# Decay phases of a linear attention: one integer-shift pass per unit in place of a per-tile subtraction, the absolute value in a buffer of its own, the modality turn planned later

## The chip, the cores and the metric

The kernel runs on one core of a Trainium2 chip (trn2). The metric is the device time of one launch in microseconds (us); the median of three runs of the kernel before is 974.35 us, from 973.89 to 974.85. The engines are named as in the profile: PE is TensorE's matmuls and PEld its weight loads, DVE is VectorE, ACT is ScalarE, POOL is GpSimd and SP is SyncE, which issues DMAs. L529 is line 529 of the kernel.

## The reference

Three stages run one after the other: a linear attention with a complex decay (4 batches, 8 heads, 768 steps, head size 48), a mixture of experts that sends each of 3072 tokens to one of 8 experts, and a dense gated layer. Cut to what matters:

```python
def _attn_ref(q, k, v, a_re, a_im):
    mag = np.sqrt(a_re * a_re + a_im * a_im)
    scale = np.minimum(mag, 0.999) / (mag + 1e-06)
    a_re_n, a_im_n = (a_re * scale, a_im * scale)
    for t in range(S):
        ar, ai = (a_re_n[:, :, t, :, None], a_im_n[:, :, t, :, None])
        new_re = ar * S_re - ai * S_im
        new_im = ar * S_im + ai * S_re
        kv = np.einsum('bhd,bhe->bhde', k[:, :, t], v[:, :, t])
        S_re, S_im = (new_re + kv, new_im)
        y[:, :, t] = np.einsum('bhd,bhde->bhe', q[:, :, t], S_re)

def _moe_ref(x, modality_id, w_gate, modality_bias, w1, w2):
    logits = x @ w_gate + modality_bias[modality_id]
    e_idx = np.argmax(logits, axis=1)
    ...
    h = np.maximum(x[mask] @ w1[e], 0.0)
    out[mask] = gate_w[mask, None] * (h @ w2[e])

def _moe2_ref(x, w_gate, w_val, w_out):
    g = x @ w_gate
    return (g / (1.0 + np.exp(-g)) * (x @ w_val)) @ w_out
```

The kernel doesn't step through time. It sums the logarithm of the decay's size and its angle over time, so that the state between two steps is a product of exponentials, cosines and sines of those sums.

## The kernel before

**Tiles and units.** The attention part works on 24 tiles (b, t): batch b and a chunk t of 128 steps, in the order of t, with the batches inside. `CUTS` groups them into eleven units of 1, 2, 3, 3, 3, 3, 3, 2, 2, 1 and 1 tiles. A tile has 384 columns (8 heads of 48), so a pass over a unit is 384, 768 or 1152 columns wide. Each unit runs through these stages, one function for each:

- `stage_a1` (L414): ACT squares `ai` into `sx`; DVE forms the magnitude (L422), counts values under a bound into `jk` (L425; only the count is used) and sums (L430); ACT takes two logarithms (L433, L436).
- `stage_a2`: ACT's exponentials (L451, and `w` at L454), DVE's ratio and clamp (L457, L460) and the decay's logarithm into `sx` (L464).
- `stage_angle`: ACT's arctangent (L478), in place in `ai`.
- `stage_decay`: PE sums the logarithms over time with a triangular matrix (L489), ACT's exponentials `p` and `r` (L492); the last row of `p` goes through a DMA (L504) and a turn on PE (L507) to `pt` (L510), the decay of a whole chunk.
- `stage_sum` (L516): the phases. For each tile, the phase at the end of the batch's chunk before it is added to the first row of the angles by a DMA that Pool issues (L526). PE sums the angles over time (L529). ACT writes the nearest whole number of turns into `ki` (L533), and DVE subtracts 2 pi times that number (L538) into `tw`. The last row of `tw` goes to DRAM by another DMA of Pool, the carry (L523).
- `stage_trig`: DVE clamps `tw` to just within plus and minus pi, in place (L562); ACT's sine (L565); DVE's absolute value, in place (L571); ACT's cosine (L575), as the sine of pi/2 minus it. So the clamp waits until the carry's DMA has read `tw`, the absolute value waits for the sine, and the cosine for the absolute value.
- `stage_prod`: k times r and q times p (L588), then the products with cosine and sine, `K` and `Q` (L597).
- `attend`: the new state (L614, L621), transposes on PE (L643) and copies on ACT (L380: `tK`, `tQ`, `yT`, `xo`), scores (L656), mask (L661), outputs (L670) and the logits (L684).
- `route`: DVE's choice of an expert (L750 to L758), counts on PE (L769, L771), ranks (L783 to L787) and the scatter by Pool (L794).

**What sets the order.** Each stage gives its instructions to a planner, `Plan`, with an engine, a cost, what they read and write, and, for DMAs, a latency (`lat`). `shapes` says how many buffers each name has. The planner orders all engines' instructions by list scheduling, the earlier in the program first, and emits them at the end; each engine then runs its list strictly in that order. Squares are fixed to ACT, absolute values to DVE and the turn counts to ACT. The costs and latencies in the planner are numbers of its own; they change the order alone.

**Modality.** `load_const` loads the tokens' modality numbers and the biases. A cast on DVE (L1104), a turn on PE (L279) and five passes on DVE (L289 to L293) make `bias`, which the routing of the first unit reads at L750.

**After it.** The first expert's slot (PE L976 and L990, DVE L983, ACT L979) begins while the attention ends; the other seven slots and the dense layer follow, and the change doesn't touch them.

Of the kernel before, what the change touches and what calls it, by code (L numbers as in the profile page):

```python
# [189 lines left out]
def tile_kernel(  # L190
# [130 lines left out]
    units = [order[sum(CUTS[:i]) : sum(CUTS[: i + 1])] for i in range(len(CUTS))]  # L321
    NU = len(units)
    cnt = const.tile([P, NU], F32, name="cnt")
    bad = const.tile([P, 2], F32, name="bad")
# [17 lines left out]
    for r in range(2):  # L342
# [6 lines left out]
        ar=(3, WIDE), ai=(4, WIDE), sx=(3, WIDE), w=(1, WIDE), q=(2, WIDE), k=(2, WIDE), v=(2, [P, CM, H, HB]),  # L349
        p=(1, WIDE), r=(1, WIDE), tw=(1, WIDE), tr=(1, [P, CM, H, 2, D]), jk=(1, WIDE, BF16), ki=(2, [P, DM], I32),  # L350
        tK=(4, [D2, 4, P]), tQ=(5, [D2, 4, P]), am=(3, [P, 4, P]), K2=(2, [P, H, 2, D]),
# [7 lines left out]
    earlyp = early.enter_context(tc.tile_pool(name="earlyp", bufs=1, side="right"))  # L359
    EARLY = ("ar", "ai", "sx", "w", "tw", "jk", "ki")  # L360
    bufs = {}
# [51 lines left out]
    def stage_a1(u):  # L413
        W = len(units[u]) * DM  # L414
        sq, sx, ai, jk = ("ar", u), ("sx", u), ("ai", u), ("jk", u)
# [24 lines left out]
        plan.op("DVE", t_dve(W), f_bad, r=sqs + [sx], w=[jk, ("cnt", u)], new=[("jk", jk)])  # L440
        plan.op("DVE", t_dve(W), f_sum, r=sqs, w=[sx])
        plan.op("ACT", t_act(W), f_la, w=sqs + ["ACT"], table=LOGEXP)
        plan.op("ACT", t_act(W), f_lx, w=[sx, "ACT"], table=LOGEXP)

    def stage_a2(u):
# [21 lines left out]
        plan.op("ACT", t_act(W), f_ri, w=ris + ["ACT"], table=LOGEXP)  # L467
        plan.op("ACT", t_act(W), f_w, r=[sx], w=[w, "ACT"], new=[("w", w)], table=LOGEXP)
        plan.op("DVE", t_dve(W), f_rt, r=ris, w=ais)
# [46 lines left out]
    def stage_sum(u):  # L516
        la, tw = ("ai", u), ("tw", u)
        for c, (b, t) in enumerate(units[u]):
            pk, ck, kk = ("ph", b, t), ("carry", b), ("ki", b, t)
            lc, tc_ = la + (c,), tw + (c,)  # L520

            def f_carry(c=c, b=b):
                gp.dma_start(carry[b], plan[tw][P - 1 : P, c, :])  # L523

            def f_add(c=c, b=b):
                gp.dma_start(plan[la][0:1, c, :], carry[b], accum_op=ALU.add)  # L526

            def f_mm(c=c, pk=pk):
                pe.matmul(plan[pk][:, :DM], tri, plan[la][:, c, :], start=True, stop=True)  # L529

            def f_ki(e, pk=pk, kk=kk):
                if e == "ACT":
                    sc.activation(out=plan[kk], in_=plan[pk][:, :DM], func=AF.Copy, scale=1.0 / TWO_PI)  # L533
                else:
                    ve.tensor_scalar(out=plan[kk], in0=plan[pk][:, :DM], scalar1=1.0 / TWO_PI, scalar2=None, op0=ALU.mult)
# [7 lines left out]
            plan.op("PE", 0.65, f_mm, r=[lc], w=[pk], new=[("B", pk), ("ki", kk)] + ([("tw", tw)] if c == 0 else []))  # L543
            plan.op({"DVE": t_dve(DM), "ACT": t_act(DM)}, 0, f_ki, r=[pk], w=[kk], kind="ki")
            plan.op("DVE", t_dve(DM), f_tw, r=[pk, kk], w=[tc_])
            if t < NC_ - 1:
                plan.op("Pool", 1.0, f_carry, r=[tc_], w=[ck], lat=3.0)

    def stage_trig(u):
        n = len(units[u])  # L550
        W = n * DM
        tw, tr = ("tw", u), ("tr", u)
        tws = each("tw", u)
# [3 lines left out]

        def angles():
            return flat(tw).rearrange("p (a d) -> p a d", d=D)

        def f_cl():
            ve.tensor_scalar(out=flat(tw), in0=flat(tw), scalar1=3.1415925, scalar2=-3.1415925, op0=ALU.min, op1=ALU.max)  # L562

        def f_sn():
            sc.activation(out=part(1), in_=angles(), func=AF.Sin)  # L565

        def f_abs(e):
            if e == "ACT":
                sc.activation(out=flat(tw), in_=flat(tw), func=AF.Abs)
# [7 lines left out]
        plan.op("DVE", t_dve(W, True), f_cl, w=tws)  # L577
        plan.op("ACT", t_act(W), f_sn, r=tws, w=[tr + (1,), "ACT"], new=[("tr", tr)], table=TRIG)
        plan.op({"DVE": t_dve(W, True), "ACT": t_act(W)}, 0, f_abs, w=tws, kind="abs")
        plan.op("ACT", t_act(W), f_cs, r=tws, w=[tr + (0,), "ACT"], table=TRIG)  # L580

# [534 lines left out]
    plan.op("DVE", 0.5, flag_2, r=["sum"], w=["bad"])  # L1116
    gone = [k for u in range(NU) for nm in EARLY for k in [(nm, u)] + each(nm, u)] + [("ki", *bt) for bt in order]
    plan.op("SP", 0.0, make_room, w=["room"], past=gone)
# [493 lines left out]
```

## Time and profile before

| what | value |
|---|---|
| median of 3 runs | 974.35 us (973.89 to 974.85) |
| the profiled execution, its own time | 973.59 us |
| its span in the trace | 971.8 us |
| PE busy | 913.3 us (94%) |
| PEld busy | 868.8 us (89%) |
| DVE busy | 606.6 us (62%) |
| ACT busy | 458.1 us (47%) |
| POOL busy | 115.6 us (12%) |

The profile is one execution, and all times of the trace count from the start of its span. The page cuts the span into 40 slices of 24 us: PE is busy for 20, 60 and 80 to 90% in the first slices and for 90% or more in most of the later ones. The attention part takes the first 280 us or so. An entry of the trace gives the start, the duration, the engine and line, the operation, and in brackets the idle time of the engine just before with what ended it.

### The profile page before, as it was taken

How to read it: one execution, taken by the hardware profiler on the slowest of the kernel's cores; microseconds unless marked ns; L12 is line 12 of the kernel's file. 1: busy time of each engine (PE TensorE's matmuls, PEld its weight loads, DVE VectorE, ACT ScalarE, POOL GpSimd, SP SyncE). 2: the span in 40 equal slices, each digit the busy share in tenths (PEclk: the TensorE clock that was granted, in tenths of full speed). 3: DMA queues.
4: the chain of work that ended last, by engine and by line, in shares of the span. 5: the costliest groups of instructions: out<-in, count | busy, mean ns of one | idle time of the engine just before them, and what ended most of it. 6: DMA issues, size and time to landing. Idle time of an engine off the chain costs nothing. (4 is left out here: it accounts for less than half of the span.)

```text
span 971.8 us, 15775 instructions
## 1 busy us (share of the span) xinstructions
PE 913.3 (94%) x5982; PEld 868.8 (89%) x5982; DVE 606.6 (62%) x1215; ACT 458.1 (47%) x798; POOL 115.6 (12%) x212
## 2 busy tenths in 40 slices
PE   2687999999988999999998899999999999999997
PEld 1466888988878999999997799999999999999996
DVE  6789989887775888788868843434333343433332
ACT  6787888786664555545444332322222232222222
POOL 2122022231220011111100010000101000010101
PEclk9887999999999999999999999999999999999999
DMA  9997365547422557333221000000000000000000
GB/s 170 161 183 142 74 132 101 101 100 206 117 65 75 95 97 215 78 78 88 55 67 49 1 25 1 1 25 1 25 1 26 1 9 17 1 25 1 25 1 25
DMA packets 155670, 64.57 MB, mean 66 GB/s; under 512 B 135564, under 2 KB 150212, under 8 KB 155588
## 3 DMA queue, kind: packets, MB, share of 16 engines
q1 hardware_dynamic: 147588, 39.82, 21.9%
q0 software_dynamic: 8000, 23.69, 9.2%
q8 instruction: 48, 0.79, 0.4%
q14 instruction: 34, 0.28, 0.1%
HBM read 67.86 MB, written 14.37 MB: 85 GB/s over the span
## 5 line engine op out<-in xcount | busy, mean ns | idle before, releaser
L1537 PE MATMUL po<-w,hd 128*128 128x384 f32 x864 | 168.9, 339 | 6.5 <-ACT hd L1420 6.4
L1517 PE MATMUL pg<-xb,w 128*128 128x384 f32 x864 | 166.1, 336 | 1.3 <-ACTq L1481 1.3
L1517 PE MATMUL pv<-xb,w 128*128 128x384 f32 x864 | 165.5, 336 | 0.0
L1537 PEld LDWEIGHTS po<-w,hd 128*128 128x128 f32 x864 | 150.4, 188 | 11.9 <-ACT hd L1420 9.1
L1521 DVE TENSOR_TENSOR sg<-sg,pg 128x384 f32<-128x384 f32 x96 | 53.2, 554 | 164.6 <-ACT sg L1520 164.6
L1517 PEld LDWEIGHTS pg<-xb,w 128*128 128x128 f32 x864 | 152.1, 188 | 1.6 <-ACTq L1481 1.6
L1517 PEld LDWEIGHTS pv<-xb,w 128*128 128x128 f32 x864 | 151.2, 188 | 0.0
L1420 ACT CAST hd<-sg 128x384 fp32r<-128x384 f32 x96 | 49.3, 513 | 161.3 <-DVE sg L1522 161.3
L1520 ACT ACTIVATE sg<-pg 128x384 f32<-128x384 f32 x96 | 47.2, 491 | 162.5 <-PE pg L1517 162.5
L1421 DVE TENSOR_TENSOR hd<-sg,hd 128x384 fp32r<-128x384 f32 x96 | 53.6, 558 | 55.6 <-ACT hd L1420 55.6
L1522 DVE TENSOR_TENSOR sg<-sg,pv 128x384 f32<-128x384 f32 x96 | 53.2, 554 | 37.3 <-PE pv L1517 36.3
L1544 POOL DMA_INDIRECT out_dram<-o,idu x24 | 23.1, 964 | 410.4 <-ACT o L1542 407.3
L976 PE MATMUL banks<-xh,w1h 128*128 128x396 f32 x192 | 67.0, 349 | 2.3 <-DVEq L1226 2.3
L979 ACT ACTIVATE hh<-banks 128x396 fp32r<-128x396 f32 x64 | 32.1, 502 | 76.0 <-PE banks L976 74.0
L976 PE MATMUL banks<-xh,w1l 128*128 128x396 f32 x192 | 66.2, 345 | 0.0
L983 DVE SCALAR_TENSOR_TENSOR hl<-banks,hh 128x396 fp32r<-128x396 f32 x64 | 36.3, 567 | 31.5 <-ACT hh L979 31.0
L656 PEld LDWEIGHTS banks<-tQ,tK 96*128 96x128 f32 x384 | 48.2, 196 | 5.2 <-issue 2.4
L656 PE MATMUL banks<-tQ,tK 96*128 96x128 f32 x384 | 52.2, 284 | 0.5 <-ACT tQ L380 0.4
L990 PE MATMUL banks<-hl,w2h 128*128 128x396 f32 x192 | 47.9, 344 | 1.2 <-DVE hl L983 1.2
L990 PE MATMUL banks<-hh,w2h 128*128 128x396 f32 x192 | 47.8, 343 | 0.3 <-ACT hh L979 0.3
L990 PE MATMUL banks<-hh,w2l 128*128 128x396 f32 x192 | 47.7, 343 | 0.0
L976 PE MATMUL banks<-xl,w1h 128*128 128x396 f32 x192 | 45.6, 346 | 0.0
(216 smaller groups left out, 1556.4 us busy)
## 6 DMA issues: line engine op xcount, KB each, us to landing
st<-in_moe_w_dram SPq DMA_DIRECT2D x64, 384.0 KB
xrows<-zero SPq DMA_DIRECT2D x8, 597.1 KB
xg<-xrows SPq DMA_DIRECT2D x8, 597.1 KB
ar<-in_a_re_dram SPq DMA_DIRECT2D x24, 192.0 KB
ai<-in_a_im_dram SPq DMA_DIRECT2D x24, 192.0 KB
q<-in_q_dram SPq DMA_DIRECT2D x24, 192.0 KB
k<-in_k_dram SPq DMA_DIRECT2D x24, 192.0 KB
v<-in_v_dram SPq DMA_DIRECT2D x24, 192.0 KB
```

The costliest lines, as they stand in the source:

```text
L656: pe.matmul(plan[ap][:, i * P : (i + 1) * P], plan[kt][:, i, :], plan[qt][:, i, :], start=True, stop=True)
L976: pe.matmul(ps[:, :SLOT], a[:, g, o : o + P], x[:, g, :], start=(n == 0), stop=(n == 3 * G3 - 1))
L979: sc.activation(out=hidden(s, f)[0], in_=ps[:, :SLOT], func=AF.Relu)
L983: ve.scalar_tensor_tensor(out=hl, in0=ps[:, :SLOT], scalar=0.0, in1=hh.bitcast(F32), op0=ALU.max, op1=ALU.subtract)
L990: pe.matmul(pds[:, g, :SLOT], w[:, f % 2, g * P : (g + 1) * P], x, start=(f == 0 and term == 0), stop=(f == KF1 - 1 and term == 2))
L1420: sc.copy(dst[0], src)
L1421: ve.tensor_tensor(out=dst[1], in0=src, in1=dst[0].bitcast(F32), op=ALU.subtract)
L1517: pe.matmul(p_, a[:, g, :], x[:, g, :n_], start=(n == 0), stop=(n == 3 * G3 - 1))
L1520: sc.activation(out=sg, in_=ps[0], func=AF.Sigmoid)
L1521: ve.tensor_tensor(out=sg, in0=sg, in1=ps[0], op=ALU.mult)
L1522: ve.tensor_tensor(out=sg, in0=sg, in1=ps[1], op=ALU.mult)
L1537: pe.matmul(p_[:, :DM], h[:, sl], w, start=(f == 0 and i == 0), stop=(f == KF2 - 1 and i == 2))
```

## The change

- The buffers `ki` and `jk` go. ACT writes each tile's phase, scaled by 2^25 / (2 pi) and rounded to int32, straight into `tw`. Per unit, DVE then shifts these integers left by 7 bits (L548), which drops whole turns by overflow, and converts them to float radians with one factor (L552).
- The clamp goes. The factor is a little under pi / 2^31, so that the result stays within plus and minus pi.
- The carries (L560) are still one DMA per tile, but stand behind the whole unit's conversion.
- The absolute value (L584) writes a buffer of its own, `ta`, one for the full width, and the cosine (L588) reads `ta`.
- The count of small values writes its unused result into the single buffer `w` (L430), which the decay's logarithm reads (L469).
- The planner's figures for `load_const` go from cost 2 to 3 and from latency 6 to 8.

Lines from L320 on move by 4 to 12: L422 becomes L426, L457 becomes L462, L529 becomes L531 and so on.

```diff
     shapes = dict(
...
-        p=(1, WIDE), r=(1, WIDE), tw=(1, WIDE), tr=(1, [P, CM, H, 2, D]), jk=(1, WIDE, BF16), ki=(2, [P, DM], I32),
+        p=(1, WIDE), r=(1, WIDE), tw=(1, WIDE), ta=(1, WIDE), tr=(1, [P, CM, H, 2, D]),
...
+    SHL = 7
+    TURN = 2.0 ** (32 - SHL)
+    RAD = 3.1415925 / 2.0**31
...
         def f_bad():
-            ve.scalar_tensor_tensor(out=flat(jk), in0=flat(sq), scalar=X_MIN, in1=flat(sx), op0=ALU.subtract,
+            ve.scalar_tensor_tensor(out=flat(w), in0=flat(sq), scalar=X_MIN, in1=flat(sx), op0=ALU.subtract,
                                     op1=ALU.is_lt, accum_out=cnt[:, u : u + 1])
...
-        plan.op("DVE", t_dve(W), f_bad, r=sqs + [sx], w=[jk, ("cnt", u)], new=[("jk", jk)])
+        plan.op("DVE", t_dve(W), f_bad, r=sqs + [sx], w=[w, ("cnt", u)], new=[("w", w)])
...
-            def f_ki(e, pk=pk, kk=kk):
-                if e == "ACT":
-                    sc.activation(out=plan[kk], in_=plan[pk][:, :DM], func=AF.Copy, scale=1.0 / TWO_PI)
...
-            def f_tw(c=c, pk=pk, kk=kk):
-                ve.scalar_tensor_tensor(out=plan[tw][:, c, :], in0=plan[kk], scalar=-TWO_PI, in1=plan[pk][:, :DM],
-                                        op0=ALU.mult, op1=ALU.add)
...
+            def f_tw(e, c=c, pk=pk):
+
+                if e == "ACT":
+                    sc.activation(out=plan[tw][:, c, :].bitcast(I32), in_=plan[pk][:, :DM], func=AF.Copy, scale=TURN / TWO_PI)
...
+        def f_shl():
+
+            ve.tensor_scalar(out=flat(tw).bitcast(I32), in0=flat(tw).bitcast(I32), scalar1=SHL, scalar2=None,
+                             op0=ALU.logical_shift_left)
+
+        def f_rad():
+            ve.tensor_scalar(out=flat(tw), in0=flat(tw).bitcast(I32), scalar1=RAD, scalar2=None, op0=ALU.mult)
+
+        W = len(units[u]) * DM
+        plan.op("DVE", t_dve(W, True), f_shl, w=each("tw", u))
+        plan.op("DVE", t_dve(W, True), f_rad, w=each("tw", u))
+        for c, (b, t) in enumerate(units[u]):
 
             def f_carry(c=c, b=b):
                 gp.dma_start(carry[b], plan[tw][P - 1 : P, c, :])
...
-        def f_cl():
-            ve.tensor_scalar(out=flat(tw), in0=flat(tw), scalar1=3.1415925, scalar2=-3.1415925, op0=ALU.min, op1=ALU.max)
...
-                ve.tensor_scalar(out=flat(tw).bitcast(I32), in0=flat(tw).bitcast(I32), scalar1=0x7FFFFFFF, scalar2=None,
+                ve.tensor_scalar(out=flat(ta).bitcast(I32), in0=flat(tw).bitcast(I32), scalar1=0x7FFFFFFF, scalar2=None,
                                  op0=ALU.bitwise_and)
 
         def f_cs():
-            sc.activation(out=part(0), in_=angles(), func=AF.Sin, scale=-1.0, bias=halfpi)
...
+            sc.activation(out=part(0), in_=angles(ta), func=AF.Sin, scale=-1.0, bias=halfpi)
...
-            plan.op("SP", 2.0, load_const, r=[("v", 0, 0)], w=["const"], lat=6.0)
+            plan.op("SP", 3.0, load_const, r=[("v", 0, 0)], w=["const"], lat=8.0)
```

The order of the instructions changes on every engine. Three places follow; a name with a number is one of the buffers of that name, `banks` is PSUM, and what stands to the left of `<-` is written. On DVE, behind the products of unit 0, before:

```order
L510 COPY pt_206<-banks 96x8
L422 SCALAR_TENSOR_TENSOR ar_157<-ar_157 128x1152
L1104 CAST modc<-modi 24x128
L457 TENSOR_TENSOR ai_162<-ai_162,ar_159 128x1152
L460 TENSOR_SCALAR ai_162<-ai_162 128x1152
L289 COPY modf<-banks 128x4x6
L290 TENSOR_TENSOR bias<-modf,mb 128x192
L291 TENSOR_SCALAR modf<-modf 128x24
L292 TENSOR_TENSOR btmp<-modf,mb 128x192
L293 TENSOR_TENSOR bias<-bias,btmp 128x192
L464 SCALAR_TENSOR_TENSOR sx_166<-sx_166,w_167 128x1152
```

and in the changed kernel:

```order
L462 TENSOR_TENSOR ai_162<-ai_162,ar_159 128x1152
L515 COPY pt_204<-banks 96x8
L465 TENSOR_SCALAR ai_162<-ai_162 128x1152
L469 SCALAR_TENSOR_TENSOR sx_166<-sx_166,w_167 128x1152
L548 TENSOR_SCALAR tw_176<-tw_176 128x768
L552 TENSOR_SCALAR tw_176<-tw_176 128x768
L633 TENSOR_TENSOR S_195<-banks,pt_204 96x8x48
L584 TENSOR_SCALAR ta_177<-tw_176 128x768
L426 SCALAR_TENSOR_TENSOR ar_157<-ar_157 128x1152
L1116 CAST modc<-modi 24x128
```

Unit 2's ratio, clamp and logarithm (L462 to L469) now stand ahead of unit 3's magnitude (L426) and of the modality cast, with unit 1's two new passes and its absolute value between them.

On ACT, from the arctangent of unit 2 to the logarithm of unit 3, before:

```order
L478 ACTIVATE ai_162<-ai_162 128x1152
L380 COPY yT_202<-banks 128x512
L380 COPY xo_204<-banks 128x384
L565 ACTIVATE tr_177<-tw_176 128x16x48
L575 ACTIVATE tr_177<-tw_176,halfpi 128x16x48
L177 ACT_TABLE_LOAD
L433 ACTIVATE ar_157<-ar_157,tiny 128x1152
```

and in the changed kernel:

```order
L483 ACTIVATE ai_162<-ai_162 128x1152
L578 ACTIVATE tr_178<-tw_176 128x16x48
L588 ACTIVATE tr_178<-ta_177,halfpi 128x16x48
L388 ACTIVATE sx_164<-ai_163 128x1152
L384 COPY yT_200<-banks 128x512
L536 ACTIVATE tw_176<-banks 128x384
L384 COPY xo_202<-banks 128x384
L536 ACTIVATE tw_176<-banks 128x384 x2
L177 ACT_TABLE_LOAD
L438 ACTIVATE ar_157<-ar_157,tiny 128x1152
```

Sine and cosine of unit 1 move ahead of the copies `yT` and `xo`, and the three `tw` writes of unit 2 (two of tiles whose first row gets a carry added) move ahead of unit 3's logarithm.

On Pool, the carries and additions around unit 4, before:

```order
L523 DMA carry_233<-tw_176 1x16x24
L526 DMA ai_160<-carry_234 1x16x24
L526 DMA ai_160<-carry_235 1x16x24
L526 DMA ai_160<-carry_236 1x16x24
L523 DMA carry_234<-tw_176 1x16x24
L523 DMA carry_235<-tw_176 1x16x24
L790 COPY xo_204<-tok 128x3
L523 DMA carry_236<-tw_176 1x16x24
```

and in the changed kernel, of units 3 and 4:

```order
L560 DMA carry_233<-tw_176 1x16x24
L560 DMA carry_234<-tw_176 1x16x24
L560 DMA carry_231<-tw_176 1x16x24
L802 COPY xo_203<-tok 128x2
L528 DMA ai_160<-carry_232 1x16x24
L528 DMA ai_160<-carry_233 1x16x24
L528 DMA ai_160<-carry_234 1x16x24
```

Before, a unit's carries leave in two goes with other work between them; now the three of a unit leave together, and the additions of the next unit follow.

## Rows read from the trace of the kernel before

**Rows 1.** Windows of 25 us: busy us (instructions) per engine, granted clock, DMA share, GB/s

```profile
core 0: us, PE busy (x) PEld busy (x) DVE busy (x) ACT busy (x) POOL busy (x), PEclk, DMA share, GB/s
...
25.00:50.00 25.00, 16.70 (x94) 11.94 (x93) 20.40 (x38) 19.54 (x26) 2.59 (x4) 0.80 1.12 166
...
75.00:100.00 25.00, 20.61 (x157) 18.10 (x156) 22.66 (x37) 19.31 (x31) 6.73 (x11) 0.80 0.66 121
100.00:125.00 25.00, 25.00 (x241) 21.74 (x239) 23.17 (x42) 21.68 (x35) 3.54 (x6) 1.00 0.50 98
```

**Rows 2.** Waits of PE, 24 to 100 us: waited for, us in total, times, longest

```profile
PE banks L643 <- ACT r L492: 4.5, 2, 2.7
PE banks L279 <- DVE modc L1104: 3.9, 1, 3.9
...
PE banks L529 <- DMA v<-in_v_dram: 1.6, 1, 1.6
```

**Rows 3.** Waits of PE, 100 to 250 us, all of them

```profile
PE banks L529 <- DVE tw L538: 0.6, 1, 0.6
PE banks L529 <- DMA ai<-carry: 0.5, 1, 0.5
PE banks L643 <- ACT tK L380: 0.3, 1, 0.3
```

**Rows 4.** Groups on DVE: busy us, mean ns, idle before; the second L571 one width alone

```profile
L538 DVE SCALAR_TENSOR_TENSOR tw<-ki,banks 128x384 f32<-128x384 int32 x24 | 12.7, 548 | 1.1 <-ACT ki L533 1.1
L588 DVE TENSOR_TENSOR k<-k,r 128x1152 f32<-128x1152 f32 (+2 forms) x11 | 11.3, 1025 | 0.3 <-ACT r L492 0.3
L562 DVE TENSOR_SCALAR tw<-tw 128x1152 f32<-128x1152 f32 (+2 forms) x11 | 6.8, 616 | 2.2 <-DMA carry<-tw 2.1
L571 DVE TENSOR_SCALAR tw<-tw 128x1152 int32<-128x1152 int32 (+2 forms) x11 | 6.5, 589 | 0.6 <-ACT tr L565 0.6
L571 DVE TENSOR_SCALAR tw<-tw 128x1152 int32<-128x1152 int32 x5 | 3.8, 751 | 0.0
```

**Rows 5.** Timeline of ACT: start, us, line, operation, idle before

```profile
21.36 0.84 ACT L478 ACTIVATE ai<-ai 128x768 f32<-128x768 f32 x1
24.91 0.52 ACT L565 ACTIVATE tr<-tw 128x384 f32<-128x384 f32 x1 [2.70 <-DVE tw L562]
...
27.79 1.26 ACT L433 ACTIVATE ar<-ar,tiny 128x1152 f32<-128x1152 f32 x1
...
39.73 1.16 ACT L478 ACTIVATE ai<-ai 128x1152 f32<-128x1152 f32 x1
...
49.41 1.26 ACT L433 ACTIVATE ar<-ar,tiny 128x1152 f32<-128x1152 f32 x1
...
267.17 0.62 ACT L575 ACTIVATE tr<-tw,halfpi 128x384 f32<-128x384 f32 x1 [1.47 <-DVE tw L571]
```

**Rows 6.** Timeline of DVE, same columns

```profile
31.48 1.36 DVE L422 SCALAR_TENSOR_TENSOR ar<-ar 128x1152 f32<-128x1152 f32 x1 [3.08 <-DMA ar<-in_a_re_dram]
...
51.78 0.17 DVE L783 TENSOR_TENSOR rank<-banks,brow 128x8 f32<-128x8 f32 x1
...
52.80 1.36 DVE L457 TENSOR_TENSOR ai<-ai,ar 128x1152 f32<-128x1152 f32 x1 [0.20 <-ACT ar L451]
...
84.83 0.95 DVE L597 TENSOR_TENSOR Q<-q,tr 128x768 f32<-128x768 f32 x1
```

**Rows 7.** Waits of POOL, 24 to 250 us

```profile
POOL ai L526 <- ACT ai L478: 29.9, 6, 13.3
...
POOL ai L526 <- DMA carry<-tw: 0.8, 1, 0.8
```

**Rows 8.** DMA issues, 0 to 100 us: queue, count, KB each, median us to landing

```profile
carry<-tw POOLq DMA_DIRECT2D x9, 1.5 KB, 3.9
ai<-carry POOLq DMA_DIRECT2D x8, 1.5 KB, 4.5
```

**Rows 9.** Timeline of PE at the attention's end

```profile
280.07 0.17 PE L769 MATMUL banks<-o,tris 128*128 128x8 bf16 x1 [2.06 <-DVE o L758]
```

More of the change, by code (lines that the diff above doesn't have):

```diff
@@ L359, in tile_kernel @@
     earlyp = early.enter_context(tc.tile_pool(name="earlyp", bufs=1, side="right"))
-    EARLY = ("ar", "ai", "sx", "w", "tw", "jk", "ki")
+    EARLY = ("ar", "ai", "sx", "w", "tw", "ta")
     bufs = {}
@@ L414, in stage_a1 @@
         W = len(units[u]) * DM
-        sq, sx, ai, jk = ("ar", u), ("sx", u), ("ai", u), ("jk", u)
+        sq, sx, ai, w = ("ar", u), ("sx", u), ("ai", u), ("w", u)
         sqs = each("ar", u)
@@ L467, in stage_a2 @@
         plan.op("ACT", t_act(W), f_ri, w=ris + ["ACT"], table=LOGEXP)
-        plan.op("ACT", t_act(W), f_w, r=[sx], w=[w, "ACT"], new=[("w", w)], table=LOGEXP)
+        plan.op("ACT", t_act(W), f_w, r=[sx], w=[w, "ACT"], table=LOGEXP)
         plan.op("DVE", t_dve(W), f_rt, r=ris, w=ais)
@@ L518, in stage_sum @@
         for c, (b, t) in enumerate(units[u]):
-            pk, ck, kk = ("ph", b, t), ("carry", b), ("ki", b, t)
+            pk, ck = ("ph", b, t), ("carry", b)
             lc, tc_ = la + (c,), tw + (c,)
-            def f_carry(c=c, b=b):
-                gp.dma_start(carry[b], plan[tw][P - 1 : P, c, :])
             def f_add(c=c, b=b):
@@ L529, in f_mm @@
                 pe.matmul(plan[pk][:, :DM], tri, plan[la][:, c, :], start=True, stop=True)
-            def f_ki(e, pk=pk, kk=kk):
+            def f_tw(e, c=c, pk=pk):
                 if e == "ACT":
-                    sc.activation(out=plan[kk], in_=plan[pk][:, :DM], func=AF.Copy, scale=1.0 / TWO_PI)
+                    sc.activation(out=plan[tw][:, c, :].bitcast(I32), in_=plan[pk][:, :DM], func=AF.Copy, scale=TURN / TWO_PI)
                 else:
-                    ve.tensor_scalar(out=plan[kk], in0=plan[pk][:, :DM], scalar1=1.0 / TWO_PI, scalar2=None, op0=ALU.mult)
@@ L537, in f_tw @@
-            def f_tw(c=c, pk=pk, kk=kk):
-                ve.scalar_tensor_tensor(out=plan[tw][:, c, :], in0=plan[kk], scalar=-TWO_PI, in1=plan[pk][:, :DM],
-                                        op0=ALU.mult, op1=ALU.add)
+                    ve.tensor_scalar(out=plan[tw][:, c, :].bitcast(I32), in0=plan[pk][:, :DM], scalar1=TURN / TWO_PI,
+                                     scalar2=None, op0=ALU.mult)
             if t > 0:
                 plan.op("Pool", 1.0, f_add, r=[ck], w=[lc], lat=3.0)
-            plan.op("PE", 0.65, f_mm, r=[lc], w=[pk], new=[("B", pk), ("ki", kk)] + ([("tw", tw)] if c == 0 else []))
@@ L544, in stage_sum @@
-            plan.op({"DVE": t_dve(DM), "ACT": t_act(DM)}, 0, f_ki, r=[pk], w=[kk], kind="ki")
-            plan.op("DVE", t_dve(DM), f_tw, r=[pk, kk], w=[tc_])
+            plan.op("PE", 0.65, f_mm, r=[lc], w=[pk], new=[("B", pk)] + ([("tw", tw)] if c == 0 else []))
+            plan.op({"DVE": t_dve(DM), "ACT": t_act(DM)}, 0, f_tw, r=[pk], w=[tc_], kind="ki")
+        def f_shl():
+            ve.tensor_scalar(out=flat(tw).bitcast(I32), in0=flat(tw).bitcast(I32), scalar1=SHL, scalar2=None,
+                             op0=ALU.logical_shift_left)
@@ L546, in stage_sum, with f_carry @@
+        def f_rad():
[4 more added lines that the diff above has]
+        for c, (b, t) in enumerate(units[u]):
+            def f_carry(c=c, b=b):
+                gp.dma_start(carry[b], plan[tw][P - 1 : P, c, :])
             if t < NC_ - 1:
-                plan.op("Pool", 1.0, f_carry, r=[tc_], w=[ck], lat=3.0)
+                plan.op("Pool", 1.0, f_carry, r=[tw + (c,)], w=[("carry", b)], lat=3.0)
@@ L551, in stage_trig @@
         W = n * DM
-        tw, tr = ("tw", u), ("tr", u)
+        tw, tr, ta = ("tw", u), ("tr", u), ("ta", u)
         tws = each("tw", u)
@@ L556, in part, with angles @@
             return plan[tr].rearrange("p c h r d -> p (c h) r d")[:, : n * H, i, :]
-        def angles():
-            return flat(tw).rearrange("p (a d) -> p a d", d=D)
-        def f_cl():
-            ve.tensor_scalar(out=flat(tw), in0=flat(tw), scalar1=3.1415925, scalar2=-3.1415925, op0=ALU.min, op1=ALU.max)
+        def angles(key):
+            return flat(key).rearrange("p (a d) -> p a d", d=D)
         def f_sn():
-            sc.activation(out=part(1), in_=angles(), func=AF.Sin)
+            sc.activation(out=part(1), in_=angles(tw), func=AF.Sin)
         def f_abs(e):
             if e == "ACT":
-                sc.activation(out=flat(tw), in_=flat(tw), func=AF.Abs)
+                sc.activation(out=flat(ta), in_=flat(tw), func=AF.Abs)
             else:
-                ve.tensor_scalar(out=flat(tw).bitcast(I32), in0=flat(tw).bitcast(I32), scalar1=0x7FFFFFFF, scalar2=None,
+                ve.tensor_scalar(out=flat(ta).bitcast(I32), in0=flat(tw).bitcast(I32), scalar1=0x7FFFFFFF, scalar2=None,
                                  op0=ALU.bitwise_and)
         def f_cs():
-            sc.activation(out=part(0), in_=angles(), func=AF.Sin, scale=-1.0, bias=halfpi)
-        plan.op("DVE", t_dve(W, True), f_cl, w=tws)
+            sc.activation(out=part(0), in_=angles(ta), func=AF.Sin, scale=-1.0, bias=halfpi)
         plan.op("ACT", t_act(W), f_sn, r=tws, w=[tr + (1,), "ACT"], new=[("tr", tr)], table=TRIG)
-        plan.op({"DVE": t_dve(W, True), "ACT": t_act(W)}, 0, f_abs, w=tws, kind="abs")
-        plan.op("ACT", t_act(W), f_cs, r=tws, w=[tr + (0,), "ACT"], table=TRIG)
+        plan.op({"DVE": t_dve(W, True), "ACT": t_act(W)}, 0, f_abs, r=tws, w=[ta], new=[("ta", ta)], kind="abs")
+        plan.op("ACT", t_act(W), f_cs, r=[ta], w=[tr + (0,), "ACT"], table=TRIG)
     def stage_prod(u):
@@ L1116, in tile_kernel @@
     plan.op("DVE", 0.5, flag_2, r=["sum"], w=["bad"])
-    gone = [k for u in range(NU) for nm in EARLY for k in [(nm, u)] + each(nm, u)] + [("ki", *bt) for bt in order]
+    gone = [k for u in range(NU) for nm in EARLY for k in [(nm, u)] + each(nm, u)]
     plan.op("SP", 0.0, make_room, w=["room"], past=gone)
```

## The prediction

> **What bounds the kernel now.** I read the windows first, then who waits for whom on TensorE, then the rows of the other engines in the stretch where TensorE waits. The windows split the attention part in two [rows 1]. From 100 us on TensorE (PE) is full, 25.00 us busy in 25.00 at a granted clock of 1.00, and in the 150 us that follow it waits 1.4 us in all [rows 3]. Between 25 and 100 us it isn't: 16.70 and 20.61 busy us in two of the windows, with a granted clock of 0.80, a mix of its two levels, 2.4 and 1.2 GHz [rows 1]. There it waits by name for ACT's `r` (4.5 us), for the modality cast on DVE (3.9) and for one phase sum (1.6) [rows 2]. DVE and ACT are at 20.40 and 19.54 of 25 in the same stretch [rows 1], so neither is full; each waits for the other in a chain of short steps. So the kernel has a start of some 90 us that is bound by the chain of DVE and ACT, and everything behind it is bound by TensorE. A gain in the start pulls all the later work forward, if the later part still keeps TensorE full. A gain on DVE in the later part is worth nothing while PE waits 1.4 us there. The last visible stall before the long fixed part is 2.06 us [rows 9].
>
> **The change part by part.** *DVE's work.* Out go 24 tile passes, 12.7 us, and eleven clamps, 6.8 us [rows 4]. In come two passes for each of eleven units. The integer shift has the form of the old absolute value: 6.5 us for all eleven, 0.751 at the full width [rows 4]. The second pass reads int32 and writes float in place, which no row shows. Its bounds are that short price, 6.5, and the price of a pass over two sources, 11.3 for eleven [rows 4], 1.36 at the full width [rows 6]; nothing in it can make it less than the shift. I take 6.5, because it is the same kind of instruction as the shift, with one source and four-byte elements. DVE's sum is 13.0 - 12.7 - 6.8 = -6.5 us; by the long price -1.7. Neither is time at the end, for the reason above: it counts only in the start.
>
> The price of that second pass is what the trace leaves open. The Trainium skill ("VectorE: DVE Perf Modes", section "What auto-detection actually checks") gives the faster mode to a pass with a single source and destination in SBUF and names no condition that the two types be equal. By it the pass costs as the shift does, and the time stays as forecast; the rows at equal types agree (0.751 against 1.36), and no row here shows the mixed one.
>
> *ACT's work.* It writes each tile's turn count as before, now into `tw`; the price is that of the old `ki` pass and no pass is added. So 0. Its new wait is that a unit's `tw` must have been read by the carry transfers, the sine and the absolute value of the unit before; behind it on ACT would stand copies of `tK`, `tQ` and the next unit's logarithms. A carry lands 3.9 us after its issue [rows 8] and the next unit's first write stands some 15 us later, so I put it at 0. Its upper bound is the 2.1 us that the old clamps waited for carries [rows 4]; a gain is excluded, since nothing on ACT is taken away.
>
> *First unit.* This is the first place with a gain. Before, the sine waited 2.70 us for the clamp, which waited for the carry to leave [rows 4, 5]. The arctangent ahead of it ends at 21.36 + 0.84 = 22.20. Now `tw` needs no clamp, so the sine follows at 22.20; 0.52 for it, 0.6 for the cosine, 1.28 for the table, and the logarithm of unit 2 starts at 24.6 to 24.7 where it started at 27.79 [rows 5]: -3.1. DVE's next step stood behind a load until 31.48 [rows 6]; in the new order that step (L426) comes after unit 2's chain, so DVE can take up the earlier start.
>
> *Unit 3's logarithm.* It started at 49.41 [rows 5]. Now it stands on ACT behind the `tw` writes of unit 2, two of which need carry additions. The arctangent of unit 2 ended before at 39.73 + 1.16 = 40.89 [rows 5], now at 37.7; then 0.8 for the first issue, 4.5 until the addition lands [rows 8], 0.6 matmul, two `tw` writes at 0.45, a second issue 0.4 later and the table, 1.28, give 46.2: -3.2. So the lead of -3.1 is kept here and not extended, and the pass at 52.80 [rows 6] is at 49.6.
>
> *From there to unit 3's last product.* Before, 84.83 - 52.80 = 32.0 us [rows 6]. DVE's passes in between change as follows: three phase passes out, -1.5; one clamp out, -0.8; two passes of unit 5 at 1.36, the count into `w` and the sum behind it, now come after this stretch, since `w` has one buffer: -2.7; one magnitude pass (L422) moves in, +1.3, and rank work of five short passes at 0.17 [rows 6], +0.8; unit 2's two new passes stand ahead of the stretch, in DVE's wait for ACT's exponential, and unit 3's behind it. That is -2.9; I take -2.7, since some short waits in the stretch stay, so the lead is -5.9 at 84.83.
>
> *What is paid back.* The 2.7 us of unit 5 are only deferred. They come back in full if DVE binds after 100 us, where it is busy 23.17 of 25 [rows 1], and not at all while PE is full. PE's full window and its 1.4 us of waits are the nearer row; I take +1.0 of the 2.7.
>
> *The modality turn later.* TensorE waited 3.9 us for the cast [rows 2], at a time when DVE itself stood for a load until 31.48 [rows 6]; what PE would have done behind it, the transposes of tile 0, now stands ahead of the turn. That removes a PE wait in the start, but the chain of DVE and ACT set the pace there, so I count 0 beside the steps above; a gain up to 3.9 lies inside the fourth case below. No DMA is moved by it: the load of the constants stands where it stood in SP's queue.
>
> *Absolute value in its own buffer.* Cosine and sine no longer take turns at `tw`; the units' later trig steps are off the bound. In the tail, the last unit's cosine waited 1.47 us for it at 267.17 [rows 5], some 13 us ahead of TensorE's 2.06 us wait for the routing of that unit [rows 9]. Between 0 and 1.47 I take 0.5, nearer to 0, since other work of DVE lies in between.
>
> *Sum:* -5.9 + 1.0 - 0.5 = -5.4 us. The profiled run took 973.59, so 968.2; it stood 0.76 under the median of 974.35, so 968.95, given as 969.0.
>
> **Rivals.** *Given back (about 973.0).* The second pass costs the long price, +1.8 in the start (0.2, 0.4, 0.6 and 0.6 for units 0 to 3, by their widths), and the 2.7 come back in full: -5.9 + 2.7 + 1.8 = -1.4, and 974.35 - 1.4 = 973.0. For it: DVE at 23.17 of 25 [rows 1]. Against it: TensorE's waits there name DVE only for 0.6 us [rows 3]. That the edits don't do what they say, and merely exchange one wait for another of the same length in the first unit, gives the same time and is counted here.
>
> *Slower (about 980).* Carries of a unit of three tiles now leave only after the third tile's write and both passes; before, each tile's carry left behind its own pass. The next unit's phase sums wait for the additions, and TensorE for those. The price is the 1.6 us that one such sum waited [rows 2]. If each of the seven units 2 to 8 pays it, 7 x 1.6 = 11.2, less 5.4, is +5.8: 980.1. It breaks even at four such stalls (6.4) and is slower by my bound from five. For it: the loop of carries is serial, 3.9 + 4.5 us in each unit [rows 8]. Against it: Pool's additions waited 29.9 us for the arctangent, 5.0 each time, and only 0.8 for a carry [rows 7], so a carry may come some 5 us later before an addition is late.
>
> A rule speaks for this rival. The Trainium skill ("SBUF — State Buffer", section "Who interferes with whom") says that a VectorE pass in its two-port mode shuts GpSimd out of the port pair, so that a transfer issued from GpSimd waits for it. Here the two new passes stand right ahead of the carries; by the rule a carry would be held by one more pass, and the price of one stall would rise from 1.6 to 1.6 + 0.75. The old clamps and absolute values were of that form too, and no row of before shows a carry held by one.
>
> *More (about 964).* PE's waits for `r` [rows 2] go as well, and the stretch at 0.80 clock from 75 to 100 us [rows 1], where PE stood before the clock fell, runs at the full level: a fifth of 25 us, 5.0, on top of 5.4, is -10.4 and 964.0. Against it: the products still wait for ACT's cosine.
>
> **How the numbers follow.** 0.2% is 1.95 us, about what a measurement here can tell from no change. Forecast 0.52, more 0.10, given back 0.22, slower 0.16. Faster is 0.52 + 0.10 = 0.62, same 0.22, slower 0.16. The range takes in the fourth case and the given-back one with one stall of 1.6 more: 963.0 to 975.0; it leaves out the slower case and a little.
>
> **What would show it.** Right: unit 2's logarithm near 24.7, the pass of unit 3 near 49.6, the last product of unit 3 near 79, PE's waits after 100 us under 3 us, both new passes at 0.75 at full width. Wrong: a second pass at 1.35; phase sums waiting for additions in several units; new PE waits after 100 us for DVE's `K` or `S`, or a start that leads by 6 us at 85 and by less than 2 at 300.

## The result, and the profile after

The changed kernel takes 961.5 us (median of 4 runs, 959.64 to 963.57) against 974.29 us for the kernel before: a ratio of 0.9865 with a 95% interval of 0.985 to 0.9879, that is 12.8 us or 1.3% faster. Beside the last experiments it took 962.86 us against 975.56, a ratio of 0.9883 (0.985 to 0.9916). The profiled execution took 962.37 us with a span of 960.6, which is 11.2 us shorter than the span of before. The forecast was 969.0 us, with a range from 963.0: the sign is right, the gain is more than twice as large as forecast, and the time lies 1.5 us below the range.

The windows of the changed kernel, with the columns of [rows 1]:

```profile
core 0: us, PE busy (x) PEld busy (x) DVE busy (x) ACT busy (x) POOL busy (x), PEclk, DMA share, GB/s
0.00:25.00 25.00, 7.59 (x11) 2.69 (x11) 18.25 (x35) 19.30 (x25) 4.88 (x30) 1.00 1.20 167
25.00:50.00 25.00, 20.91 (x138) 16.62 (x137) 21.89 (x40) 22.07 (x32) 4.33 (x8) 1.00 1.02 167
50.00:75.00 25.00, 19.28 (x146) 14.84 (x147) 24.20 (x43) 22.65 (x36) 4.51 (x6) 0.95 1.17 188
75.00:100.00 25.00, 25.00 (x204) 22.42 (x205) 21.00 (x37) 21.44 (x33) 4.04 (x7) 0.78 0.65 109
100.00:125.00 25.00, 25.00 (x257) 22.75 (x254) 22.76 (x45) 21.93 (x36) 10.39 (x14) 1.00 0.67 137
```

From 25 to 50 us TensorE is busy for 20.91 us at full clock; before it was 16.70 us at 0.80 [rows 1]. From 75 to 100 us it is full, at 0.78. Its waits from 24 to 100 us, all of them, beside [rows 2]:

```profile
PE banks L655 <- ACT r L497: 4.9, 2, 4.5
PE banks L696 <- ACT yT L384: 1.4, 2, 0.7
PE banks L682 <- DVE am L673: 1.2, 1, 1.2
PE banks L626 <- DVE S L633: 1.2, 1, 1.2
PE banks L626 <- ACT tw L536: 0.7, 1, 0.7
```

The waits for the modality cast (3.9 us) and for a phase sum's input (1.6 us) are gone, and so are two that [rows 2] leaves out:

```profile
PE banks L614 <- DVE K L597: 2.6, 2, 1.7
PE banks L769 <- DVE o L758: 2.6, 1, 2.6
```

The wait for `r` is still there. And from 100 to 250 us, beside [rows 3]:

```profile
PE banks L531 <- DVE pos L798: 0.8, 1, 0.8
PE banks L655 <- DVE K L609: 0.4, 1, 0.4
```

The steps of the start, on ACT and then on DVE (start, us, line), beside [rows 5] and [rows 6]:

```profile
21.33 0.84 ACT L483 ACTIVATE ai<-ai 128x768 f32<-128x768 f32 x1
22.08 0.51 ACT L578 ACTIVATE tr<-tw 128x384 f32<-128x384 f32 x1
22.50 0.60 ACT L588 ACTIVATE tr<-ta,halfpi 128x384 f32<-128x384 f32 x1
...
24.41 1.25 ACT L438 ACTIVATE ar<-ar,tiny 128x1152 f32<-128x1152 f32 x1
...
44.83 1.27 ACT L438 ACTIVATE ar<-ar,tiny 128x1152 f32<-128x1152 f32 x1
```

```profile
27.80 1.36 DVE L462 TENSOR_TENSOR ai<-ai,ar 128x1152 f32<-128x1152 f32 x1 [2.00 <-ACT ar L456]
...
33.13 1.35 DVE L426 SCALAR_TENSOR_TENSOR ar<-ar 128x1152 f32<-128x1152 f32 x1
...
49.32 1.36 DVE L462 TENSOR_TENSOR ai<-ai,ar 128x1152 f32<-128x1152 f32 x1
...
75.20 0.95 DVE L609 TENSOR_TENSOR Q<-q,tr 128x768 f32<-128x768 f32 x1
```

Sine and cosine follow the arctangent without a gap, and the logarithm of unit 2 starts at 24.41 (27.79 before). Unit 2's ratio starts at 27.80; before it stood behind the magnitude of unit 3, which waited for its load until 31.48 and held it until 32.89. Unit 3's magnitude now comes at 33.13 and waits for nothing. Unit 3's logarithm is at 44.83 (49.41), its ratio at 49.32 (52.80), and the product that the prediction calls unit 3's last at 75.20 (84.83): a lead of 9.6 us there, and of 11.2 at the end. That product is the sixth tile's, so it is unit 2's last; the same instruction is compared in both kernels.

The price that the trace of before left open, by form on DVE (busy us, mean ns):

```profile
L552 DVE TENSOR_SCALAR tw<-tw 128x1152 f32<-128x1152 int32 x5 | 3.8, 757 | 0.1
L548 DVE TENSOR_SCALAR tw<-tw 128x1152 int32<-128x1152 int32 x5 | 3.8, 754 | 0.0
```

The pass from int32 to float costs 757 ns at the full width, as much as the shift.

### The profile page after: what moved, and what is told of

Same layout as the page of the kernel before. It is cut to its first block, busy times and chain, and to the rows that moved or that the text cites. A ratio compares the mean times of both kernels' runs of the same rounds, so it can differ in the third digit from the quotient of the medians.

```text
span 960.6 us, 15805 instructions
## 1 busy us (share of the span) xinstructions
PE 911.9 (95%) x5982; PEld 870.2 (91%) x5982; DVE 600.9 (63%) x1202; ACT 457.5 (48%) x798; POOL 117.7 (12%) x212
```

## The experiments

The theories. A: the gain starts with the sine and cosine of the first units, which no longer wait for carries, and grows because DVE no longer stands for unit 3's load ahead of unit 2's ratio. B: the modality turn at the head of TensorE's queue held the transposes and is worth what the prediction missed.

**Parts put back, order kept.** The planner orders everything anew after any edit, so in these four kernels its finished list is kept, and one pass is put in or a few instructions are moved.

*The clamp ahead of the sine:*

```diff
         def f_sn():
+            ve.tensor_scalar(out=flat(tw), in0=flat(tw), scalar1=3.1415925, scalar2=-3.1415925, op0=ALU.min, op1=ALU.max)
             sc.activation(out=part(1), in_=angles(tw), func=AF.Sin)
```

> The changed kernel, with the old clamp put back on VectorE ahead of each unit's sine: it writes the phases in place, so it waits for the unit's carries to land, and the sine waits for it. The order of everything else is kept. Theory A (the sine freed from the clamp starts the lead, 3.4 us at unit 2's logarithm, and all later gains hang on it): the logarithm of unit 2 goes back from 24.4 to about 27.8 and 3 to 6 us of the 12.8 are lost: 965 to 968. Theory B (the later modality turn, which unblocks TensorE's queue, is worth most): no more than 1 to 2 us are lost: about 963.

976.85 us (ratio to the kernel before 1.0026, 1.0013 to 1.004): all of the gain is gone and 2.6 us more. The clamps on DVE, all eleven, and the first unit's sine on ACT:

```profile
L578 DVE TENSOR_SCALAR tw<-tw 128x1152 f32<-128x1152 f32 (+2 forms) x11 | 6.6, 597 | 7.6 <-DMA carry<-tw 7.6
```

```profile
25.09 0.52 ACT L579 ACTIVATE tr<-tw 128x384 f32<-128x384 f32 x1 [2.72 <-DVE tw L578]
```

The sine waits 2.72 us again, as in [rows 5], and DVE stands 7.6 us for carries where it stood 2.1 [rows 4]. The carries of a whole unit leave late now. That is harmless in the changed kernel because nothing on DVE writes `tw` behind them before the next unit.

*The load first:*

```diff
+        rt = find("f_rt", 2)
...
+        ahead(load, rt)
+        ahead(find("f_sq", 3), rt)
+        ahead(find("f_cast"), rt)
```

`load` issues the inputs of unit 3; it has to stand ahead of the magnitude in the list, and SyncE's own order stays as it was.

> The changed kernel, with unit 3's magnitude and the modality cast put back ahead of unit 2's ratio on VectorE, as they stood before; the rest of the order is kept. Theory A2 (VectorE no longer stands for the load of unit 3, which lands at about 31.5 in both kernels, and this extends the lead from 3.4 to 5.1 us): unit 2's ratio goes back from 27.8 to about 32.9 and 4 to 5 us are lost: 965.5 to 966.5. If the gain came through TensorE's queue or from the clamp alone: under 1.5 us lost, 961.5 to 963.

968.85 us (0.9943, 0.9926 to 0.9959): 7.35 us of the 12.8 are lost, more than expected. DVE in this kernel:

```profile
31.99 1.36 DVE L436 SCALAR_TENSOR_TENSOR ar<-ar 128x1152 f32<-128x1152 f32 x1 [5.82 <-DMA ar<-in_a_re_dram]
33.26 0.21 DVE L1127 CAST modc<-modi 24x128 f32<-24x128 int32 x1
33.40 1.34 DVE L472 TENSOR_TENSOR ai<-ai,ar 128x1152 f32<-128x1152 f32 x1
```

DVE stands 5.82 us for the load, and unit 2's ratio is back at 33.40 where it was 27.80. The wait is longer than the 3.08 of [rows 6] because the sine is early: what the one edit gives, this wait takes. What stands behind the load in DVE's list holds the other engines too. The copy `pt` comes at 34.66, TensorE's transposes wait for it, and ACT's copy of them waits 2.98 us for TensorE:

```profile
PE banks L665 <- DVE pt L525: 2.9, 1, 2.9
```

Unit 3's ratio is at 56.12 here, against 49.32 in the changed kernel and 52.80 in the kernel before.

*The modality turn alone, early:*

```diff
+        ahead(find("f_cast"), find("f_rt", 2))
+        ahead(find("turn_modi"), find("f_t"))
+        ahead(find("make_bias"), find("f_ln", 2))
```

> The changed kernel, with only the modality turn put back early: its cast ahead of unit 2's ratio on VectorE, its turn on TensorE ahead of the first transposes of tile 0, and its bias passes ahead of unit 2's last logarithm pass; the rest of the order is kept. Theory A (the turn's place is worth little beside the chain of ACT and VectorE; only its passes of 1.6 us move ahead in VectorE's queue): 961.5 to 963.5. Theory B (the turn at the head of TensorE's queue held the transposes and cost what the prediction missed, some 5 us): 965 to 967.

962.32 us (0.9876, 0.9859 to 0.9892): no difference from the changed kernel. Theory B falls.

*A pass twice:*

```diff
         def f_rad():
+            ve.tensor_scalar(out=flat(tw).bitcast(I32), in0=flat(tw).bitcast(I32), scalar1=0, scalar2=None,
+                             op0=ALU.logical_shift_left)
```

> The changed kernel, with one more pass of VectorE per unit between the two new ones (a shift by 0, in place): 6.5 us more work of VectorE in all, 1.8 us of it in units 0 to 3; the order is kept. If VectorE's work counts only in the start: 961.5 + 1.8 = 963.3. If VectorE also sets the pace behind 100 us: up to 961.5 + 6.5 = 968. If VectorE is nowhere the bound: 961.5.

964.58 us (0.9895, 0.9878 to 0.9913): 3.1 us for 6.5 us of DVE's work. So a part of it counts; the two intervals together leave some 1 to 5 us. In its trace unit 4's logarithm is 2.0 us later than in the changed kernel, and that is still 1.9 at unit 10's; nothing accumulates behind 100 us until the tail.

**Parts put back, planned anew.** Theory C is what is left of A: the gain rests on the free sine and on unit 2's ratio standing first.

```diff
-            plan.op("SP", 3.0, load_const, r=[("v", 0, 0)], w=["const"], lat=8.0)
+            plan.op("SP", 2.0, load_const, r=[("v", 0, 0)], w=["const"], lat=6.0)
```

> The changed kernel, with the planner's old figures for the load of the modality constants (cost 2, latency 6), so that it plans the turn early again, and all else anew. Unit 2's ratio still stands ahead of unit 3's magnitude on VectorE and the sine is free of the clamp. Theory C (the gain rests on these two): 961.5 to 963.5. Rival (the later turn is a good part of the 12.8 us): 965 or more.

961.27 us (0.986, 0.9827 to 0.9893): nothing lost. The planner's new figures are worth nothing in the changed kernel.

```diff
-                ve.tensor_scalar(out=flat(ta).bitcast(I32), in0=flat(tw).bitcast(I32), scalar1=0x7FFFFFFF, scalar2=None,
+                ve.tensor_scalar(out=flat(tw).bitcast(I32), in0=flat(tw).bitcast(I32), scalar1=0x7FFFFFFF, scalar2=None,
...
-            sc.activation(out=part(0), in_=angles(ta), func=AF.Sin, scale=-1.0, bias=halfpi)
+            sc.activation(out=part(0), in_=angles(tw), func=AF.Sin, scale=-1.0, bias=halfpi)
```

> The changed kernel, with the absolute value written back into the phases, so that it waits for the sine and the cosine waits for it; planned anew. The sine is still free of the carries. Theory C: some 0.5 to 1 us for each of the first three or four units, 963 to 965. Rival (the buffer of its own carries the gain, as it lets the cosine and the next logarithm start early): 967 or more.

965.86 us (0.9906, 0.9872 to 0.9941): 4.4 us lost, more than expected. ACT in the first unit:

```profile
22.38 0.51 ACT L578 ACTIVATE tr<-tw 128x384 f32<-128x384 f32 x1
24.85 0.61 ACT L588 ACTIVATE tr<-tw,halfpi 128x384 f32<-128x384 f32 x1 [1.96 <-DVE tw L584]
...
27.15 1.25 ACT L438 ACTIVATE ar<-ar,tiny 128x1152 f32<-128x1152 f32 x1
```

The sine is early, but the absolute value overwrites `tw`, so it waits for the sine and the carry, and the cosine waits 1.96 us for it. Unit 2's logarithm is at 27.15, nearly where it was before. So without the buffer of its own little of the first unit's lead is left. Yet 8.4 of the 12.8 us of gain remain in this kernel, so the early sine is not the root of the whole gain, as theory A has it.

*The count's own buffer,* with the absolute value in place:

```diff
-            ve.scalar_tensor_tensor(out=flat(w), in0=flat(sq), scalar=X_MIN, in1=flat(sx), op0=ALU.subtract,
+            ve.scalar_tensor_tensor(out=flat(jk), in0=flat(sq), scalar=X_MIN, in1=flat(sx), op0=ALU.subtract,
```

> The changed kernel with the absolute value in place, and with the count's result in a buffer of its own again; planned anew. It is to be set beside the run with the absolute value in place alone (965.9). Theory C: 965 to 967, the count's buffer is worth nothing. Rival (the prediction's third step, 2.7 us of counts and sums deferred): 968.5.

965.95 us (0.9905, 0.9882 to 0.9928), against 965.86 without it: the buffer of the count is worth nothing.

**Parts put into the kernel before.** First the planner's figures alone, then with the count in `w`:

> The kernel before, with the planner's new figures for that load alone. The planner then puts unit 2's ratio ahead of unit 3's magnitude, so VectorE no longer stands for the load of unit 3 until 31.5 us; the ratio can start when its exponential is there, at 31.2 where it was 32.9, and the clamp stays. Theory C: a gain of 1.7 to 3 us, 971 to 972.5. Rival (the later turn is worth much by itself): 966 to 969.

969.16 us (0.9946, 0.9926 to 0.9966).

> The kernel before, with two parts of the change: the count's unused result goes into the single buffer of the decay's exponential, and the turn is planned later. The per-tile subtraction, the clamp and the absolute value in place stay. Theory C: as with the turn alone (969.2), within 1.5 us, since the clamp and the absolute value still wait for the carries: 968 to 971. Rival (the count in that buffer, which keeps a unit's count and sum later, gives a good part of the lead as the prediction's third step has it, 2.7 us): 966.5.

968.64 us (0.9938, 0.9918 to 0.9959). So the figures alone give 5.3 us on the kernel before, which theory C did not expect, and the count again nothing beyond the noise. Three kernels looked for what in the new order gives it, each in the order of before with one or two moves:

```diff
+        sq, ln = find("f_sq", 3), find("f_ln", 2)
+        seq.remove(sq)
+        seq.insert(seq.index(ln) + 1, sq)
```

> The kernel before, in its own order, with one instruction moved: unit 3's magnitude goes behind unit 2's three passes on VectorE (ratio, clamp, logarithm), so that these no longer stand behind the load. Theory C: unit 2's ratio at 31.2 instead of 32.9 and a gain of 1.7 to 3 us, 971 to 972.5, as in the kernel with the turn alone; the rest needs the earlier sine. Rival (the load's place alone is worth the 7.4 us that its return cost in the changed kernel): 967 to 968.

975.61 us (1.0014, 0.9997 to 1.003): nothing, though unit 2's ratio starts at 30.31. Its windows, with the columns as above:

```profile
25.00:50.00 25.00, 19.12 (x97) 13.75 (x96) 20.52 (x38) 19.26 (x25) 2.60 (x4) 0.77 1.07 163
50.00:75.00 25.00, 23.97 (x152) 19.41 (x152) 20.70 (x37) 19.80 (x33) 5.86 (x9) 0.75 1.16 181
75.00:100.00 25.00, 19.12 (x160) 16.57 (x159) 23.29 (x42) 20.31 (x32) 6.75 (x11) 0.86 0.66 127
```

TensorE is busy for longer than before from 25 to 75 us, at a lower granted clock (0.77 and 0.75, against 0.80 and 0.93 in the kernel before). The other two move unit 0's counts behind unit 2's phase sums on TensorE, without and with the move above:

```diff
+        cnt = find("f_cnt", 0)
...
+        seq.remove(cnt)
+        seq.insert(seq.index(sums[-1]) + 1, cnt)
```

> The kernel before in its own order, with one thing moved: on TensorE, the counts of unit 0's routing go behind the two phase sums of unit 2 that stood behind them. Theory E (this wait of 2.6 us is what the later turn removes): 969 to 971. Rival (the sums wait for their carries anyway, which land at the same time): no gain, 973.5 to 975.

> Both moves on the kernel before: the counts of unit 0 behind unit 2's phase sums on TensorE, and unit 3's magnitude behind unit 2's three passes on VectorE. Theory F (two waits that end at the same time hide each other, so only both together gain): 969 to 971, while each alone gives nothing. Rival (the clamp and the absolute value in place, which wait for carries, set the pace whatever stands ahead): 973.5 to 975.

975.17 us (1.0001, 0.9983 to 1.0019) and 975.09 us (1.0001, 0.9992 to 1.0011): nothing either, so theories E and F fall. TensorE's waits from 24 to 100 us in the first of them:

```profile
PE banks L289 <- DVE modc L1115: 4.6, 1, 4.6
PE banks L624 <- DVE K L607: 4.3, 2, 2.4
...
PE banks L779 <- DVE o L768: 0.6, 1, 0.6
```

The wait for the choice of expert is 0.6 us, and the wait for `K`, which hangs on the cosine, is 4.3. In the kernel before it was 2.6 for each of the two. So 2.0 us were taken from the one wait and 1.7 came back in the other; that the clamp and the absolute value, which hold the cosine, are the reason is argued, not shown.

**The wait for `r` that is left.** In ScalarE's list, one pair of unit 3's exponentials, or all three, ahead of unit 4's logarithms (`ln`):

```diff
+        for i in dec[:2]:
+            ahead(i, ln)
```

> The changed kernel in its own order, with one pair of ScalarE's passes moved: the exponentials p and r of the first tile of unit 3 go ahead of the logarithms of unit 4. TensorE waited 4.53 us for that r at 73.78, with the clock at 0.63 and 0.69 in the 20 us from 70 on. Theory D (the half-clock stretch behind that wait is worth several us): the wait falls to about 1 us and the time to 957 to 960. Rival (the chain of ScalarE and VectorE sets the pace, and 0.75 us are put into it): 961.5 to 962.5.

> As the run with one pair ahead, with all three pairs of unit 3 ahead of the logarithms of unit 4, 2.2 us in that chain. Theory D: no wait for r is left, the clock stays up, 957 to 960. Rival: the chain's 2.2 us are lost, 963 to 964.

964.15 us (0.989, 0.9863 to 0.9918) and 963.21 us (0.9879, 0.9858 to 0.9901), against 961.5 for the changed kernel: no gain. Theory D isn't borne out, and isn't tested as meant, since the wait didn't go. From 60 to 100 us TensorE's longest wait is, in the first and in the second:

```profile
PE banks L636 <- ACT r L507: 4.5, 1, 4.5
```

```profile
PE banks L678 <- ACT tQ L394: 4.8, 1, 4.8
```

It stands as long at the next instruction that needs ACT. ACT has no wait there between about 67 and 77 us in any of the three kernels; its logarithms, exponentials and copies come one after the other.

The changed kernel once more, beside the last two:

> The changed kernel once more, for its time beside the others of this call: 960 to 963 by its four runs so far, on this chip too.

962.86 us, as given above. No kernel tried here is faster than the changed one beyond the noise.

## Why the prediction was right and wrong

**What bounds: right.** The gain is made ahead of 100 us and kept behind it. With the four windows up to 100 us, busy time times granted clock gives a rough measure of TensorE's work done by then, at full speed: before 7.57 x 1.00 + 16.70 x 0.80 + 20.79 x 0.93 + 20.61 x 0.80 = 56.8 us, after 7.59 + 20.91 + 19.28 x 0.95 + 25.00 x 0.78 = 66.3. The two windows of before that [rows 1] leaves out:

```profile
0.00:25.00 25.00, 7.57 (x11) 2.84 (x12) 17.05 (x32) 16.59 (x22) 4.88 (x30) 1.00 1.21 167
50.00:75.00 25.00, 20.79 (x154) 16.51 (x154) 21.94 (x43) 20.97 (x33) 5.67 (x9) 0.93 1.12 184
```

The difference is 9.6 us (from unrounded values), and the span is 11.2 us shorter. Of the 9.6, 7.1 are busy time that was idle, and 2.5 are half-clock time less. The waits by name point the same way: between 24 and 100 us all of them, not only those in [rows 2], sum to 16.6 us before and 9.4 after. Each is one execution: in the trace of the changed kernel's second measurement the work is 6.6 us more than before, the waits sum to 13.0, and the span is 10.0 shorter. The measure is an estimate: in all other kernels it comes within 4 us of the difference of the spans, but for the one with the clamp put back (5.7), where TensorE also waits 5.9 us from 100 to 250.

**First unit: the size right, the cause half told.** -3.1 forecast, -3.4 measured (27.79 to 24.41), and the clamp put back returns the 2.72 us wait. But the step credited the clamp's removal, and the buffer for the absolute value was put at 0.5 us in the tail. The run with the absolute value in place shows that without this buffer the logarithm comes at 27.15 and 4.4 us of the end time go. This term was mis-sized, though it isn't where the sum went wrong.

**From unit 2's ratio to unit 3's: right at its end.** The prediction saw that DVE stood for a load until 31.48 and that the new order puts that step behind unit 2's. The lead was then 5.1 us at unit 2's ratio (32.89 to 27.80) and 4.6 at unit 3's logarithm, for 3.2 forecast. Unit 2's arctangent came 5.3 us earlier (39.73 to 34.43), since ACT's square for unit 3, 1.2 us, now stands behind the cosine and some 0.7 us of ACT's waits for transposes are gone. But unit 3's ratio has a lead of 3.5 us, 49.32 for 49.6 forecast, because it now stands behind the first tile's routing on DVE. The order is worth much, 7.35 us by the run that puts the load first again; the sum had it inside these 3.2.

**From there to the product at 84.83: the step that failed.** The prediction took 2.7 us off the 32.0 and so had a lead of 5.9. The stretch takes 25.9 us (49.32 to 75.20), 6.1 less, and the lead is 9.6. The passes moved about as counted (2.9), and one more pass, for `S`, left the stretch (0.5). What it had wrong is the waits: it reduced its 2.9 to 2.7, "since some short waits in the stretch stay", but nearly all of them went, 2.1 us. DVE's waits before, the first 0.2 us of them at the very start of the stretch:

```profile
DVE tw L538 <- ACT ki L533: 0.9, 1, 0.9
DVE am L661 <- PE banks L656: 0.6, 1, 0.6
DVE ai L457 <- ACT ar L451: 0.4, 2, 0.2
DVE l L694 <- PE banks L684: 0.4, 1, 0.4
DVE pt L510 <- PE banks L507: 0.3, 1, 0.3
```

and after:

```profile
DVE ai L462 <- ACT ar L456: 0.3, 1, 0.3
```

Most of them were waits for TensorE: three name it, and the `ki` of the first had itself stood 2.15 us for TensorE's phase sum. So TensorE held DVE there, and the prediction followed only the other direction. That TensorE was late because of its own waits ahead of 50 us is a reading; no run isolates it. In the traces of all kernels with the new phase passes this stretch takes 25.8 to 29.9 us, also with the load first (26.8), and in all with the old ones 32.0 to 33.3. So the shortening goes with the phase passes, and not with the place of the load; what each part of them gives of it wasn't tried.

**The count in `w`: the passes moved, but not for that reason.** Unit 5's count and sum did leave the stretch. They leave it as well in the two kernels planned anew in which the count has a buffer of its own (the planner's figures alone, and the absolute value in place with the count's own buffer), so the single buffer isn't the cause. Two pairs of kernels with and without it differ by 0.1 and 0.5 us at the end.

**Paid back +1.0: wrong.** Nothing was paid back; the lead of 9.6 us is 11.0 at the last routing. This term and the stretch make up the miss of the sum, -5.4 forecast and -11.2 between the two profiled executions; the small misses of the other terms cancel. An extra pass on DVE cost 3.1 us of its 6.5, with 1.8 expected if it counts only in the start, so whether DVE binds at all behind the start stays open.

**The modality turn at 0: right** for the changed kernel, by two runs (961.27 and 962.32). TensorE's 3.9 us wait for the cast did vanish, but it was the same wait as DVE's for the load, seen from TensorE. On the kernel before, the planner's new figures alone give 5.3 us through a new order; neither of the two moved instructions tried explains it, nor both, and what in the new order does it stays open.

**The second pass: right.** 757 ns at the full width against 754 for the shift; the 1.36 us price of the rival "given back" did not come. The rule of the Trainium skill ("VectorE: DVE Perf Modes", section "What auto-detection actually checks") holds here for a pass with two four-byte types that differ.

**The tail at -0.5: about 0.2.** The lead is 11.0 us at the last routing and 11.2 at the end. The last unit's cosine no longer waits, but TensorE's wait of 2.06 us for the choice of expert is the same:

```profile
269.10 0.17 PE L781 MATMUL banks<-o,tris 128*128 128x8 bf16 x1 [2.06 <-DVE o L770]
```

**The rivals.** "Slower" took its price of 1.6 us from a row of [rows 2] that names a load of `v`; the one wait for an addition was 0.5 us [rows 3]. Late carries are a real mechanism, but not where it was put: in the changed kernel TensorE has no wait for an addition from 24 to 250 us, while DVE stands 7.6 us once a clamp waits for the carries. In two other orders TensorE does wait for additions, 3.9 us with the planner's old figures (961.27 us, as fast as the changed kernel) and 4.5 with the absolute value in place. The rule cited beside it (the Trainium skill, "SBUF — State Buffer", section "Who interferes with whom") can't be seen at work here: one more such pass ahead of the carries cost 3.1 us, less than its own 6.5 us of work. "More", given 0.10 and 964, is nearest to what happened: the clock did come up. But it came up where TensorE's waits went (25 to 50 us, 0.80 to 1.00), while from 75 to 100 us it is 0.78, as low as before (0.80), and the wait for `r` that the rival thought gone is there, 4.5 us long. The fault behind these is one of method: the lead was followed on DVE's list, and TensorE's own waits, of which [rows 2] shows 10.0 us of 16.6, were not taken off one by one, nor the clock that they cost.

## What to carry to other kernels

Where two waits lie close together on a chain of in-order engines, price them together, for the gains of the parts don't add up: the whole change gave 12.8 us; with the load first again it gave 5.4 and with the absolute value in place 8.4; in the kernel before, one instruction moved so that the ratio comes first gave nothing, and the planner's figures alone, which also put it first, gave 5.3. A value that a slow reader (a DMA, another engine) still needs should not be overwritten in place on the engine that paces the stretch; a second buffer turned a chain of four steps on two engines into two steps side by side. And where the late part of a kernel is full on TensorE, measure a start by TensorE's busy time times its granted clock up to the point where it is full, beside the lead of one of its feeders; and ask of each feeder's waits whether TensorE itself is what it waits for.

## What the runs showed of the hardware

A TensorE that is busy for longer isn't always further on. In the kernel with the ratio moved first it was busy for 4.1 us longer up to 100 us than in the kernel before, and as much more was lost to half clock, 13.1 us against 8.9 (busy time times one less the granted clock, over the same four windows), so that by this measure no more work was done. Why the clock was lower there wasn't tried. Runs of one kernel differ by 4 us: of the first four of the changed kernel, 959.64 us had a granted clock of 0.992 over the run, and 963.57 us had 0.986. The clock isn't all of it, as a later run of 967.25 us had 0.986 too.
